# Cell sums and weight splits moved behind the block seams, a new order of matrix-block buffers, the last chunk's sums ahead of its value products, and kept blocks later in the sweeps

## The chip, the cores and the metric

The kernel runs on one core of one Trainium2 chip. Its engines are TensorE (PE in the rows; its weight loads are PEld), VectorE (DVE), ScalarE (ACT), GpSimd (POOL) and SyncE (SP). Each works through its own queue in order; SP issues nearly all DMA transfers here. The metric is the device time of one execution in microseconds (us), less is better. The kernel before takes 1789.12 us (median of 3 runs, 1788.32 to 1796.11). The profiled execution, from which all rows come, took 1783.08 us.

## What is computed

A sequence of 2048 rows of 640 numbers passes through four layers, each with a layer norm ahead and a residual sum behind: A, B, A, B.

```python
def _A_ref(x, wqkv, wo):          # H = 32 heads of 20, window W = 8, dilation 2
    qkv = (x @ wqkv)...           # q, k, v
    idx = pos[:, None] - off[None, :]      # off = 0, 2, ..., 14
    logits = einsum("bhsd,bhswd->bhsw", q, k[idx]) * scale
    logits = where(idx >= 0, logits, -1e9)
    o = einsum("bhsw,bhswd->bhsd", softmax(logits), v[idx])
    return o.reshape(B, S, D) @ wo
def _B_ref(x, Cr, Ci, Dr, Di):
    a, b = x @ Dr.T, x @ Di.T
    return Cr @ a - Ci @ b
x = x + _A_ref(layernorm(x), wqkv, wo)
x = x + _B_ref(layernorm(x), ...)
x = x + _A_ref(layernorm(x), wqkv, wo)
x = x + _B_ref(layernorm(x), ...)
```

## The kernel before

**Arithmetic.** Each operand of a product is split into a rounded upper half and the rest, and a product is three matmuls (`PASSES`: upper by upper and the two mixed ones). So each tile that PE multiplies costs a copy on ACT (the upper half) and a subtraction (the lower half) on DVE or POOL ("a split", L127 and L131 for weights).

**Layer A** (`layer_a`, the first at about 0 to 396 us, the second at about 860 to 1277) goes over 4 chunks `c` of 512 rows, each of 4 tiles `j`. Its order is written out by hand: `at(step, phase, fn)` puts a piece of work into one of 67 steps, and inside a step the phases run in the order of `PHASES`. All engines keep to that order. A query/key/value product (L363) is evacuated by ACT (L370, tile `stg`), stored to memory (L379, L380) and read back as windows `win` (L418) and queries `qs`; ACT copies the queries into a bank (`q_copy`, L405); DVE multiplies queries by keys (L432) and probabilities by values (L472); POOL sums the products (L435, and L491 to L493); DVE does the reductions and the softmax (L442 to L467); ACT the exponential (L450). Output tiles are transposed on PE (L328), split by ACT (L332), a subtraction on PE (`pc_sub`, L336) and ACT (L351), multiplied by the output weights (`wo_mm`, L516) and added to the residual by DVE (`wo_add`, L160), which also frees the product's bank.

**Layer B** multiplies by the sequence matrix first. Its first output tile of two (`z_mm`, L963, t = 0) is computed inside the tail of layer A: 16 blocks of the sequence matrix, of 15 matmuls each, in thirds of five that `ZTHIRDS` gives to steps. In the first layer B (`li` = 1) a block is loaded raw (`c_load`, L919), split by ACT (`c_hi`, L923) and by POOL or DVE (`c_lo`, L950); blocks that were split before are kept in memory (`c0b`) and read back (`c_get`, L941), which is what the second one does with all of them. A split block sits in one of three buffers `s0`, `s2`, `s3` in turn (`c_tag`, L912); a raw one in one of two buffers `stg`, which the evacuations of layer A use too. `run` then evacuates the first tile (`zt_put`, L1018 to L1023), loads the hidden weights (`load_w`, L127 to L131), computes the second tile block by block, and among that work forms sums of cells of the normalised input (`x_whole`, L1086, and `x_combine`, L1094 to L1097). The rest of the output is computed by three `pair`s with seven products in place of eight (L1130), each in three sweeps over `NP` = 8 blocks, whose raw blocks come from memory (L1113) and are split by L1123 and L1124. In the first layer B the last sweeps of the pairs also split and store ten blocks in all for the second one (`c_keep`, list `KEEP`).

**Between the layers.** The last pair of the first layer B runs inside the second layer A (`early`), with hooks at its last sweep that load, normalise, transpose (L226) and split (L233, L237) the first tiles and load the first weights.

**Who sets the order.** In layer A the plan does, for all engines. In `run`, `pair` and `early` only PE's order is by hand; for the other engines the framework chooses from its own forecast, and `tc.issue_after(x)` keeps what is under it behind instruction `x`.

## Time and profile before

| | |
|---|---|
| median of the runs | 1789.12 us (1788.32 to 1796.11) |
| profiled execution | 1783.08 us, span 1781.3 us, mean granted PE clock 0.995 |
| PE busy | 1740.1 us (98%), 8798 matmuls |
| DVE, ACT, POOL busy | 1386.1 (78%), 813.7 (46%), 622.1 us (35%) |
| DMA | 425.15 MB, 239 GB/s on the mean |

A row of the timeline gives start and length in us, engine, line, operation, output and input tiles, tile of the array, shape and count; in square brackets the idle time of the engine before it and the instruction or transfer that ended it. A row of a group gives, behind the count, the busy time in us and the mean in ns, then the idle time ahead of the group's instructions with what ended it. A row of stretches gives the window, its length, for each engine the busy time and the count, the granted clock of PE (1.00 is full speed), the mean busy share of the DMA engines and GB/s.

### The profile page before, as it was taken

Reading aid. Unit: us, or ns where it says so; the run is one execution under the profiler, and the core shown is the slowest. Engines: PE = TensorE matmul, PEld = TensorE weight load, DVE = VectorE, ACT = ScalarE, POOL = GpSimd, SP = SyncE. Lnnn points to the kernel's source line nnn. Section 1 sums busy time; section 2 is a strip of 40 time slices with the busy share of each in tenths; the row PEclk is TensorE's granted clock in tenths of the full one; section 3 lists DMA queues with packets and bytes.
Section 4 is the critical chain, followed back from the end, with each engine's and each line's share of the span. In section 5 each row is a group of like instructions: output and inputs, shape, how many; then the busy total and the mean of one; then the engine's idle time right before and its main releaser. Section 6 shows DMA issues by size and latency. Waiting matters only on the chain.

```text
span 1781.3 us, 26451 instructions
## 1 busy us (share of the span) xinstructions
PE 1740.1 (98%) x8798; PEld 1505.6 (85%) x8798; DVE 1386.1 (78%) x2133; ACT 813.7 (46%) x1690; POOL 622.1 (35%) x585
## 2 busy tenths in 40 slices
PE   9999998999999999999999999999899999999999
PEld 7889887778888888888888889987788888888888
DVE  6999999987867767767738999989777677677683
ACT  4664544454444445445624344444434443443441
POOL 4899999840000000000017999989200000000000
PEclk9999998999999999999999999999999999999999
DMA  7896678758777687778737866687688767767761
GB/s 248 286 313 206 212 209 281 251 180 293 265 255 256 238 271 252 244 265 257 228 117 223 273 207 224 214 299 267 212 287 277 252 219 238 258 224 231 254 207 52
DMA packets 271849, 425.15 MB, mean 239 GB/s; under 512 B 22592, under 2 KB 150592, under 8 KB 271456
## 3 DMA queue, kind: packets, MB, share of 16 engines
q1 hardware_dynamic: 268512, 421.49, 71.8%
q10 hardware_dynamic: 3200, 1.97, 0.4%
q8 instruction: 70, 1.15, 0.3%
q14 instruction: 67, 0.55, 0.1%
HBM read 338.23 MB, written 85.14 MB: 238 GB/s over the span
## 4 chain that ended last, share of the span: by engine, by line
PE 60%; DVE 18%; DMA 10%; POOL 5%; issue 4%; ACT 2%; SPq 1%; DVEq 0%; ACTq 0%; POOLq 0%
PE aux L1041 13%; PE m L363 11%; PE m L1130 10%; PE t L1130 10%; PE pq L1130 5%; PE xt L1130 5%; DVE pr L432 4%; PE aux L516 3%; DVE pr L472 3%; DMA xc<-stg 3%; DMA win<-cs_in 2%; DVE lg L442 2%; POOL pr L491 2%; POOL pr L435 1%; POOL pr L492 1%
## 5 line engine op out<-in xcount | busy, mean ns | idle before, releaser
L363 PE MATMUL m<-r,s 128*128 128x480 f32 x1920 | 436.4, 382 | 2.8 <-ACT s L233 2.3
L363 PEld LDWEIGHTS m<-r,s 128*128 128x128 f32 x1920 | 355.2, 188 | 56.6 <-ACT s L233 3.2
L1123 ACT CAST r<-win 128x512 fp32r<-128x512 f32 x248 | 151.2, 619 | 168.4 <-DVE win L1159 81.5
L1041 PE MATMUL aux<-r2a,zo 128*128 128x320 f32 x768 | 226.4, 310 | 0.0
L175 POOL TENSOR_TENSOR stats<-stats,mhalf 128x1 f32<-128x1 f32 (+1 forms) x40 | 29.2, 730 | 560.0 <-ACT stats L171 551.1
L491 POOL TENSOR_TENSOR pr<-pr 128x640 f32<-128x640 f32 x126 | 207.0, 1643 | 40.3 <-DVE pr L472 39.8
L1041 PE MATMUL aux<-pr,zo 128*128 128x320 f32 x704 | 208.2, 308 | 0.0
L1124 DVE TENSOR_TENSOR r<-win,r 128x512 fp32r<-128x512 f32 x248 | 167.5, 688 | 44.4 <-ACT r L1123 43.1
L432 DVE TENSOR_TENSOR pr<-pq,win 128x1280 f32<-128x1280 f32 x128 | 189.7, 1483 | 15.7 <-ACT pq L405 12.9
L472 DVE TENSOR_TENSOR pr<-pq,win 128x1280 f32<-128x1280 f32 x128 | 190.9, 1491 | 4.9
L435 POOL TENSOR_TENSOR pr<-pr 128x640 f32<-128x640 f32 x118 | 168.2, 1426 | 12.9 <-DVE pr L432 12.4
L1130 PE MATMUL m<-r,r 128*128 128x512 f32 x606 | 156.2, 392 | 0.7 <-DVE r L1124 0.7
L1041 PEld LDWEIGHTS aux<-r2a,zo 128*128 128x128 f32 x768 | 144.1, 188 | 2.0
L1130 PEld LDWEIGHTS m<-r,r 128*128 128x128 f32 x606 | 113.6, 188 | 26.3 <-DVE r L1124 1.0
L1041 PEld LDWEIGHTS aux<-pr,zo 128*128 128x128 f32 x704 | 132.2, 188 | 2.1
L1130 PE MATMUL t<-r,r 128*128 128x512 f32 x483 | 130.7, 393 | 2.0 <-issue 1.0
L963 PE MATMUL m<-s,r 128*128 128x512 f32 x384 | 119.3, 398 | 11.6 <-DMA s<-c0b 3.8
L963 PE MATMUL t<-s,r 128*128 128x512 f32 x384 | 118.4, 396 | 2.3 <-DVE ot L1023 1.5
L492 POOL TENSOR_TENSOR pr<-pr 128x320 f32<-128x320 f32 x126 | 112.3, 891 | 9.9
L442 DVE TENSOR_REDUCE lg<-pr 128x64 f32<-128x640 f32 (+1 forms) x128 | 110.5, 864 | 4.5 <-POOL pr L435 4.3
L1130 PEld LDWEIGHTS t<-r,r 128*128 128x128 f32 x483 | 90.5, 188 | 23.4 <-issue 1.5
L370 ACT COPY stg<-m 128x480 f32<-128x480 f32 x128 | 70.9, 554 | 81.4 <-PE m L363 61.3
(283 smaller groups left out, 3231.0 us busy)
## 6 DMA issues: line engine op xcount, KB each, us to landing
win<-cs_in SPq DMA_DIRECT2D x354, 256.0 KB, 4.2
r<-xc SPq DMA_DIRECT2D x240, 256.0 KB, 4.4
win<-kvb SPq DMA_DIRECT2D x96, 440.0 KB, 4.5
xa<-cs_in SPq DMA_DIRECT2D x122, 256.0 KB, 4.3
win<-kvb SPq DMA_DIRECT2D x64, 360.0 KB, 5.0
xc<-stg SPq DMA_DIRECT2D x40, 512.0 KB, 3.4
kvb<-stg SPq DMA_DIRECT2D x60, 320.0 KB, 4.5
xr<-xs SPq DMA_DIRECT2D x41, 320.0 KB, 3.2
```

Of the source, the lines that this page charges most:

```text
L363: nc.tensor.matmul(mt[g][:, : 3 * F], st[:, a, k], wq[q][:, b, k], start=n == 0, stop=n == 14)
L432: nc.vector.tensor_tensor(pr, q, wview(u, jp, 0, [[1, FE]]), op=ALU.mult)
L435: nc.gpsimd.tensor_tensor(pv[:, :, 0:10], pv[:, :, 0:10], pv[:, :, 10:20], op=ALU.add)
L442: nc.vector.tensor_reduce(lgs[u][:, 2 * jp : 2 * jp + 2].rearrange("p j w h -> p (j w h)"), prq.pop((u, jp)), axis=AX.X, op=ALU.add,)
L472: nc.vector.tensor_tensor(pr.rearrange("p j w (h d) -> p j w h d", d=DH), lgs[u][:, 2 * jp : 2 * jp + 2].unsqueeze(4).to_broadcast([P, 2, ...
L491: g.tensor_tensor(pr[:, :, 0:4], pr[:, :, 0:4], pr[:, :, 4:8], op=ALU.add)
L492: g.tensor_tensor(pr[:, :, 0:2], pr[:, :, 0:2], pr[:, :, 2:4], op=ALU.add)
L963: self.last = nc.tensor.matmul(self.z[t][k], self.xn[c][:, a, j, k * P : (k + 1) * P], self.ct[s][:, b], start=s == 0 and i == 0, stop=s = ...
L1041: self.last = nc.tensor.matmul(self.ym[e][:, :320], zt[(k, a, ri)][:, j2 * P : (j2 + 1) * P], w[:, e * 320 : (e + 1) * 320], start=(k, a, ...
L1123: nc.scalar.copy(hi, raw)
L1124: nc.vector.tensor_tensor(lo, raw, hi.bitcast(F32), op=ALU.subtract)
L1130: nc.tensor.matmul(bank, w(a, kb), hl[b], start=start and (a, b) == (0, 0), stop=stop and (a, b) == (1, 0),)
```

## The change

No operation is added or taken away but for six weight splits that go from DVE to POOL. What changes is the place of work in the queues:

- Layer A of the first pass, step 46: the two subtractions of `pc_sub` go to a new phase `peL2` behind the output products.
- `c_tag`: the buffers of the split blocks rotate as `s2`, `s3`, `s0` in both layers.
- Block 0 in the first layer is loaded and split one step earlier; the upper half of block 3 goes to a new phase `chi` behind the copies of the output tiles. `ZTHIRDS` of the first layer gives a third of block 2 to step 52, and thirds of step 52 run ahead of that step's output products (both layers).
- Last chunk (`c` = 3): the residual loads move to step 58, `wo_add` to phase `sA` (ahead of the softmax parts and the value products on DVE), and its statistics and norms one step earlier.
- `run`: `x_whole` and `x_combine` stand behind the last evacuation of the first tile.
- `pair`: the kept blocks (up to four in a pair) are split and stored at blocks 2 to 5 of the last sweep rather than at 0 to 3.
- `early`: the transposes use other banks and hooks, and loads and splits of the weights of query groups 1 to 3 move into the plan of the second layer A, steps -7 to 1; odd ones split on POOL (`wq_split`).

```diff
@@ -44,9 +44,10 @@
 
 
 LEAD2 = (-7, -6, -5, -4, -2, -1, 0, 0, 1, 1, 2, 3, 3, 4, 5, 5)
+WSTEP = (0, 0, 0, 1, 1, 2, 2, 3, 3, 4, 4, 5, 5, 6, 7)
 WHOLE = ((43, 45, 47, 49, 51, 55, 57, 59), (51, 57))
 ZTHIRDS = (
-    {49: 3, 50: 3, 51: 2, 53: 3, 54: 1, 56: 3, 57: 6, 58: 3, 59: 4, 60: 2, 61: 1, 62: 3, 63: 4, 64: 1, 55: 0, 52: 0},
+    {49: 3, 50: 3, 51: 2, 52: 1, 53: 2, 54: 1, 56: 3, 57: 6, 58: 3, 59: 4, 60: 2, 61: 1, 62: 3, 63: 4, 64: 1},
     {50: 3, 51: 5, 52: 1, 53: 1, 54: 1, 55: 1, 56: 5, 57: 4, 58: 3, 59: 3, 60: 1, 61: 1, 62: 4, 63: 2, 64: 4},
 )
 TA = 65
@@ -301,7 +302,7 @@
                 pieces[step] = []
                 at(step, "peT0", pc_pe, step)
                 at(step, "hi", pc_hi, step)
-                at(step, "peL", pc_sub, step)
+                at(step, "peL2" if first and step == 46 else "peL", pc_sub, step)
                 at(step, "actL", pc_lo, step)
             pieces[step].append((kind, c, j, k0, k1, bank, col, tag))
 
@@ -555,6 +556,11 @@
         def wq_split(q, k):
             split(wq[q][:, 0, k], wq[q][:, 1, k], wq[(q, k)], eng=nc.gpsimd if k % 2 else None)
 
+        def wq_late(q, k):
+            if k == 0:
+                wq_begin(q)
+            wq[(q, k)] = wq_load1(q, k)
+
         def wo_raw(i):
             if i == 0:
                 wo_s["w"] = T([P, 2, KD, D], "r2a", F32R)
@@ -586,8 +592,8 @@
                 with tc.issue_after(prev.dma.ins):
                     wq[0] = a_weights_q(0)
 
-            def xt(j, part):
-                xt_pe(0, j, part, "pq")
+            def xt(j, part, bank="pq"):
+                xt_pe(0, j, part, bank)
                 xt_hi(0, j, part)
                 xt_lo(0, j, part)
 
@@ -597,17 +603,19 @@
                 {
                     2: lambda: (x_get(0), x_get(1)),
                     4: lambda: xt(0, 0),
-                    5: lambda: (xt(0, 1), x_get(2)),
-                    6: lambda: xt(1, 0),
-                    7: lambda: (w0(), xt(1, 1), x_get(3)),
-                    ("y", 1): lambda: xt(2, 0),
-                    ("y", 2): lambda: xt(2, 1),
-                    ("y", 3): lambda: xt(3, 0),
-                    ("y", 4): lambda: xt(3, 1),
+                    5: lambda: x_get(2),
+                    6: lambda: xt(0, 1),
+                    7: lambda: (w0(), xt(1, 0), x_get(3)),
+                    ("y", 0): lambda: xt(1, 1),
+                    ("y", 1): lambda: (xt(2, 0, "xt"), xt(2, 1, "t0")),
+                    ("y", 2): lambda: xt(3, 0),
+                    ("y", 3): lambda: xt(3, 1, "xt"),
                 },
             )
-            for q in range(1, NQ):
-                wq[q] = a_weights_q(q)
+            for i, (q, k) in enumerate((q, k) for q in range(1, NQ) for k in range(KD)):
+                st = LEAD2[0] + WSTEP[i]
+                at(st, "dmaw", wq_late, q, k)
+                at(st + 1, "misc", wq_split, q, k)
 
         def zero_rows():
             zrow = wtile([4, (W - 1) * FE])
@@ -788,13 +796,14 @@
                     tp(60 if j < 2 else 67, "o", c, j, 3, 5, "aux0" if j < 2 else "pq", 256 * (j % 2))
                 if j < len(w):
                     if xtags:
-                        at(w[j], "dmar", r_load, c, j, xtags[j])
+                        at(58, "dmar", r_load, c, j, xtags[j])
                     at(w[j], "pe3w", wo_mm, c, j, ("aux1", "aux0") if c == 3 else ("aux0", "aux1"))
-                    at(w[j] + 1, "misc", wo_add, c, j)
-                    at(w[j] + 2, "actl", wo_stats, c, j)
-                    at(w[j] + 3, "fin", wo_fin, c, j, j + 1)
-                    at(w[j] + 3 + (c == 2), "actl", handoff.ln_hi_own, c, j, xr, nstats)
-                    at(w[j] + 4 + (c == 2), "misc", handoff.ln_lo, c, j)
+                    d = c == 2
+                    at(w[j] + 1, "misc" if d else "sA", wo_add, c, j)
+                    at(w[j] + 1 + d, "actl", wo_stats, c, j)
+                    at(w[j] + 2 + d, "fin", wo_fin, c, j, j + 1)
+                    at(w[j] + 2 + 2 * d, "actl", handoff.ln_hi_own, c, j, xr, nstats)
+                    at(w[j] + 3 + 2 * d, "misc", handoff.ln_lo, c, j)
         for ph in ("peT0", "hi", "peL", "actL"):
             plan.pop((67, ph))
         at(66, "pe3w", wo_mm, c, 2, ("aux0", "aux1"), 0, 2, 0, 3)
@@ -818,13 +827,14 @@
             if first and z in PRE:
                 at(max(thirds[3 * z - 7] + 1, t - 3), "dmac", handoff.c_get, z)
             elif first:
+                t -= z == 0
                 at(t - 2, "dmac", handoff.c_load, z)
-                at(t - 1, "hi", handoff.c_hi, z)
+                at(t - 1, "hi" if z != 3 else "chi", handoff.c_hi, z)
                 at(t - 1, "misc", handoff.c_lo, z, z < NJ or z in (11, 12))
             else:
                 at(min(t - 1, 48 + z) if z < 3 else t - 1, "dmac", handoff.c_get, z)
             for p in range(3):
-                at(thirds[3 * z + p], "pe3", handoff.z_mm, z, p)
+                at(thirds[3 * z + p], "pe2" if thirds[3 * z + p] == 52 else "pe3", handoff.z_mm, z, p)
         if first:
             at(62, "dmac", handoff.c_load, 13)
             at(63, "hi", handoff.c_hi, 13)
@@ -833,7 +843,7 @@
             at(63, "dmac", handoff.c_get, 13)
 
         PHASES = (
-            "peT0 dma evac hi pe peL pe2 fin red0 dma2 qk sA sB av0 sD red1 sE sC exp evacA actL evacO actl sF av1 qc actz"
+            "peT0 dma evac hi pe peL pe2 peL2 fin red0 dma2 qk sA sB av0 sD red1 sE sC exp evacA actL chi evacO actl sF av1 qc actz"
             " dmaw dmas misc dmac dmar pe3w pe3"
         ).split()
         with tc.manual_schedule(engines=ENGINES):
@@ -910,9 +920,8 @@
 
         def c_tag(self, s, t=0):
             if t:
-                return (("s3", "s0") if self.li == 1 else ("s0", "s3"))[s % 2]
-            tags = ("s3", "s0", "s2") if self.li == 1 else ("s2", "s0", "s3")
-            return tags[s % 3] if s < NST - 1 else "s1"
+                return ("s3", "s0")[s % 2]
+            return ("s2", "s3", "s0")[s % 3] if s < NST - 1 else "s1"
 
         def c_load(self, s, t=0):
             self.raw[s] = T([P, 512], "stg", bufs=2)
@@ -1017,10 +1026,14 @@
             for o, r in pieces[0]:
                 nc.scalar.copy(o, z[:, r])
             if len(pieces[0]) == len(pieces[1]) == 1:
-                nc.vector.tensor_tensor(pieces[1][0][0], z, pieces[0][0][0].bitcast(F32), op=ALU.subtract)
+                self.low = nc.vector.tensor_tensor(
+                    pieces[1][0][0], z, pieces[0][0][0].bitcast(F32), op=ALU.subtract
+                )
             else:
                 for r in range(2):
-                    nc.vector.tensor_tensor(zt[(k, 1, r)], z[:, r], zt[(k, 0, r)].bitcast(F32), op=ALU.subtract)
+                    self.low = nc.vector.tensor_tensor(
+                        zt[(k, 1, r)], z[:, r], zt[(k, 0, r)].bitcast(F32), op=ALU.subtract
+                    )
 
         def evac(self, t):
             self.zt_new(t)
@@ -1247,8 +1260,8 @@
                     self.product(f2, self.x_plain(*k1(i), 512), p12, False, i == NP - 1)
                     c6 = split(combine(b11, b11, b12, ALU.add))
                     self.product(m6, x6, c6, *ends)
-                    if self.li == 1 and i < len(KEEP[p]):
-                        self.c_keep(KEEP[p][i], views, tags)
+                    if self.li == 1 and 2 <= i < 2 + len(KEEP[p]):
+                        self.c_keep(KEEP[p][i - 2], views, tags)
                     if i > 2:
                         self.ymm(t1, 0, i - 3, i - 2)
                     hook(i)
@@ -1274,7 +1287,7 @@
         def run(self, nstats):
             self.evac(0)
             self.load_w()
-            todo = []
+            low, todo = self.low, []
             for i in range(0, NP, 2):
                 todo += [(self.x_whole, (side, i)) for side in (2, 0)]
                 todo += [(self.x_combine, (m, i)) for m in XC]
@@ -1287,8 +1300,9 @@
                     if s == 13:
                         self.ymm(0, 1, 0, 2)
                     if s > 1:
-                        for fn, args in todo[:3]:
-                            fn(*args)
+                        with tc.issue_after(low.ins):
+                            for fn, args in todo[:3]:
+                                fn(*args)
                         todo = todo[3:]
                 assert not todo
                 self.ymm(0, 1, 2, KD)
```

## The prediction

> **What bounds the kernel now.** I read the page's totals first, then PE's waits, then PE in order of time round each place that the diff touches, then the other engines at those places. All line numbers are those of the kernel before.
>
> ```profile
> span 1781.3 us, 26451 instructions
> PE 1740.1 (98%) x8798; PEld 1505.6 (85%) x8798; DVE 1386.1 (78%) x2133; ACT 813.7 (46%) x1690; POOL 622.1 (35%) x585
> ```
>
> TensorE is busy 1740.1 of 1781.3 us, and the change leaves every matmul in place. So all that it can win is idle PE time, 41.2 us, and matmuls that ran at a lower clock. The idle time lies in short gaps. These are the ones at the touched places (start, length, instruction, count, then the idle time before it and its releaser):
>
> ```profile
> 263.26 0.83 PE L336 MATMUL t<-s,nident 128*128 128x256 f32 x2 [1.79 <-ACT s L332]
> 280.92 1.42 PE L963 MATMUL m<-s,r 128*128 128x512 f32 x5 [1.71 <-POOL s L950]
> 298.10 2.24 PE L516 MATMUL aux<-r2a,ot 128*128 128x320 f32 x7 [2.05 <-ACT s L351]
> 354.07 6.21 PE L516 MATMUL aux<-r2a,s 128*128 128x320 f32 x30 [2.82 <-DVE xa L160]
> 374.34 2.91 PE L516 MATMUL aux<-r2a,zo 128*128 128x320 f32 x18 [0.18 <-ACT zo L351]
> 398.96 0.94 PE L963 MATMUL t<-s,r 128*128 128x512 f32 x3 [0.75 <-DVE ot L1023]
> 400.30 0.94 PE L963 MATMUL t<-s,r 128*128 128x512 f32 x3 [0.39 <-DVE ot L1020]
> 573.78 0.49 PE L1130 MATMUL xt<-r,r 128*128 128x512 f32 x1 [0.49 <-ACT r L1123]
> 575.12 0.73 PE L1130 MATMUL xt<-r,r 128*128 128x512 f32 x2 [0.85 <-DVE r L1124]
> 583.42 1.43 PE L1130 MATMUL m<-r,r 128*128 128x512 f32 x5 [0.72 <-DVE r L1124]
> 863.51 0.55 PE L226 MATMUL pq<-ident,xa 128*128 128x128 f32 x3 [0.94 <-DVE s L237]
> 890.21 2.46 PE L363 MATMUL m<-r,s 128*128 128x480 f32 x10 [0.67 <-ACT s L233]
> 897.74 2.44 PE L363 MATMUL m<-r,s 128*128 128x480 f32 x10 [1.66 <-ACT s L233]
> 1179.19 0.73 PE L963 MATMUL m<-s,r 128*128 128x512 f32 x2 [2.58 <-DMA s<-c0b]
> 1235.30 4.67 PE L516 MATMUL aux<-r2a,s 128*128 128x320 f32 x30 [0.41 <-DVE xa L160]
> 1246.88 0.73 PE L963 MATMUL m<-s,r 128*128 128x512 f32 x2 [1.23 <-DMA s<-c0b]
> 1280.22 0.93 PE L963 MATMUL m<-s,r 128*128 128x512 f32 x3 [2.25 <-DVE zo L1023]
> 1282.62 0.93 PE L963 MATMUL t<-s,r 128*128 128x512 f32 x3 [0.76 <-DVE ot L1023]
> 1283.95 0.93 PE L963 MATMUL t<-s,r 128*128 128x512 f32 x3 [0.40 <-DVE ot L1020]
> ```
>
> The 18 gaps other than the 0.18 sum to 22.5 us, 1.3% of the run. Between these places PE runs without a pause, so what is won at one is kept. Whether a gap can be won depends on what its releaser itself waited for.
>
> **The change, place by place.**
>
> **A, first layer, 264 to 303.** By stretch (us, then busy time and count of PE, PEld, DVE, ACT, POOL, the granted clock, DMA share, GB/s), then ACT and DVE in order of time, and the group of DMA issues (count, KB each, median us to landing):
>
> ```profile
> 264.00:303.00 39.00, 33.02 (x162) 28.21 (x161) 36.62 (x53) 19.66 (x48) 35.85 (x34) 0.87 0.89 290
> ```
> ```profile
> 290.00:294.00 4.00, 2.60 (x12) 2.33 (x13) 3.93 (x6) 1.74 (x7) 3.03 (x4) 0.84 0.96 328
> ...
> 298.00:302.00 4.00, 3.90 (x15) 3.90 (x15) 3.65 (x6) 3.84 (x8) 3.84 (x4) 0.50 0.96 334
> ...
> 354.00:358.00 4.00, 3.93 (x16) 3.93 (x17) 3.93 (x8) 0.35 (x2) 3.84 (x5) 0.57 0.68 220
> ...
> 1180.00:1184.00 4.00, 4.00 (x16) 3.26 (x14) 1.81 (x3) 0.16 (x1) 3.85 (x4) 0.57 1.04 388
> ```
> ```profile
> 270.64 0.42 ACT L405 COPY pq<-qs 128x320 f32<-128x320 f32 x1
> ...
> 274.10 0.62 ACT L923 CAST s<-stg 128x512 fp32r<-128x512 f32 x1 [0.35 <-DMA stg<-cs_in]
> ```
> ```profile
> 272.16 1.48 DVE L432 TENSOR_TENSOR pr<-pq,win 128x1280 f32<-128x1280 f32 x1
> ```
> ```profile
> stg<-cs_in SPq DMA_DIRECT2D x8, 256.0 KB, 4.8
> ```
>
> Here DVE is the bound (36.62 of 39 us) and PE is not (33.02). So moving the two L336 subtractions of step 46 behind 15 products removes PE's 1.79 but shortens nothing by itself: 0. Against it stands the earlier block 0. Its load now precedes two key/value loads on SP and its cast L923 precedes the query copy L405 on ACT. The load's buffer is a store's buffer, so it cannot start sooner; the cast still waits for the landing, at 274.10. L405 then runs at about 274.7 to 275.1 rather than 270.64, and DVE's L432 at 275.1 rather than 272.16: +2.9, less some 0.5 of slack that DVE has in the 2.4 us it idles here: +2.4. Behind it on ACT wait L370 and four L332 copies, so PE idles from about 272 to 276. On SP the two key/value loads wait some 6 us for that buffer and land about as DVE needs them: 0 to 0.3. The cast's lower half on POOL (L950) moves ahead of L435 on an engine that is 35.85 of 39 busy; it removes the 1.71 and delays the sums by its 1.3, both inside DVE's bound. A third of block 2, five matmuls, moves into the gap before 298.10: -1.2, since five take 1.42 in the row at 280.92 with their drain. At 298 the clock is 0.50: seven L516 took 2.24 (0.32 each) where 18 took 2.91 at full speed (0.16 each), which doubles some 2.4 us of products. With the gaps round 290 differently spread I take 2.2 of that as saved. Sum 2.4 - 1.2 - 2.2 = -1.0. Ends: all of the delay hidden, -3.4; the load landing in its group's 4.8 instead of the 2.6 it took here, and the clock still low, 2.4 + 2.2 - 1.2 = +3.4.
>
> [...]
>
> **B, first layer, last chunk.** The sums L160 that free the product banks move ahead of the value products:
>
> ```profile
> 353.53 0.48 DVE L160 SCALAR_TENSOR_TENSOR xa<-aux,xa 128x320 f32<-128x320 f32 x1
> ```
> ```profile
> 353.69 1.55 POOL L491 TENSOR_TENSOR pr<-pr 128x640 f32<-128x640 f32 x1 [1.84 <-DVE pr L472]
> ...
> 366.27 1.93 POOL L491 TENSOR_TENSOR pr<-pr 128x640 f32<-128x640 f32 x1 [0.62 <-DVE pr L472]
> ```
>
> PE's 2.82 ahead of 354.07 goes, and the 0.57 clock after it probably, worth half of 3.4 us, 1.7. But L472 then starts two L160 later (1.0), and POOL, which sums behind it without a pause from 353.69 to some 366, becomes what PE waits for. I take -1.5. Ends -4.5 (both kept) and +1.0 (only the delay of L472). The earlier residual load costs SP two issues, under 1 us, and no one waits for them.
>
> **C and H, the two block seams (398, 1280).** The changed order puts L1086 (1.22 us on DVE) behind the last evacuation:
>
> ```profile
> 1277.82 0.74 ACT L127 ACTIVATE r2a<-xa 128x640 fp32r<-128x640 f32 x1 [2.31 <-DMA xa<-wre_in]
> ...
> 1280.59 1.22 DVE L1086 TENSOR_TENSOR s<-r 128x1024 f32<-128x1024 f32 x1
> ```
>
> Gaps 0.75 + 0.39 and 0.76 + 0.40 go: -1.1 each (ends -1.3, 0). The 2.25 stays: there ACT waits for a weight load that the change leaves where it was. What slides later is feed for pairs that start some 75 us on.
>
> **D, kept blocks at blocks 2 to 5 of a pair's last sweep, not 0 to 3.** The gaps at 573 to 583 lie in the first blocks of such a sweep. By stretch, as above:
>
> ```profile
> 570.00:580.00 10.00, 8.66 (x40) 6.76 (x40) 5.20 (x9) 3.54 (x7) 0.32 (x1) 1.00 1.02 357
> 590.00:600.00 10.00, 10.00 (x54) 8.83 (x53) 4.26 (x8) 1.72 (x4) 0.00 (x0) 1.00 0.56 185
> ```
>
> Where the gaps are, DMA is full (1.02) and DVE is not; some blocks later it is at 0.56. Moving four loads and eight stores there frees the early blocks: 0.49 + 0.85 + 0.72 = 2.1 at most; the later pairs' share I do not count. I take -1.8. Ends -2.6, and +2.5 if gaps of 0.85 come up at three later blocks.
>
> **E, early, 860 to 900.** Transposes move to other banks and one step forward, and 15 weight splits leave this stretch for layer A's plan:
>
> ```profile
> L131 DVE TENSOR_TENSOR r<-win,r 128x480 fp32r<-128x480 f32 x20 | 12.9, 657 | 6.2 <-ACT r L127 6.0
> L127 ACT ACTIVATE r<-win 128x480 fp32r<-128x480 f32 x20 | 11.8, 603 | 4.7 <-DMA win<-wqkv_in 3.6 <-PE m L1130 0.8
> ```
>
> L233 and L237, for which PE waits, no longer stand behind ACT and DVE work that waits for weights: 0.94 + 0.67 + 1.66 = -3.3. In layer A the second query group's products start near 909, its last split would end near 893 and the fourth group's near 932 against a need at 944; six go to POOL, which is idle there until 924. Ends -3.3 and -1.0.
>
> **F, G, second layer A.** The load of block 1 takes a buffer that is free about 2 us sooner, so SP issues the rest sooner, block 2's included:
>
> ```profile
> s<-c0b SPq DMA_DIRECT2D x22, 512.0 KB, 5.5
> ```
>
> Block 2 took some 6.7 us from its issue at 1172.5. Of its 2.58 I take 1.4 (ends 0 and -4.2, with the 0.57 clock behind it). In the last chunk the 0.41 goes, the 1.23 hangs on a load that stands behind the same store as before: -0.4 (ends -1.6, +1.5).
>
> **Sum.** -1.0 - 1.5 - 1.1 - 1.8 - 3.3 - 1.4 - 0.4 - 1.1 = -11.6 us. It is made on the profiled execution's 1783.08 us (span 1781.3); the median of the runs is 1789.12, 6.0 above, and I carry the difference over: 1777.5. The ends added singly are -22.2 and +7.4; as they are independent, the likeliest case's own range is 1773 to 1783.
>
> **The rivals.**
> 1. Transfers set what I give to order. Blocks 0 and 2 and the kept blocks wait for landings either way, so A, D and F give nothing: -7.4, 1781.7. For it: 0.35 and 2.58 "<-DMA", DMA share 0.89 to 1.04. Against: 0.56 after 590.
> 2. The clock never falls. B and F keep the 1.7 each, A goes to -3.4: -17.4, 1771.7. For it: the low stretches follow the gaps that go. Against: A's new idle time.
> 3. A's new idle time, 272 to 276 on PE, lowers the clock for a stretch of 3.4 us, and the 298 one stays: A is +1.2 + 1.7 = +2.9, sum -7.7, 1781.4. [...]
> 4. DVE and POOL hold A and B, and D and F return as other gaps, so only C, E, H count: -5.5, with half of E lost to late weights -3.8: 1785.3. For it: DVE 3.93 of 4 at 354.
> 5. Slower: the block load holds ACT more than once. The two store buffers are shared, so each of blocks 0 to 3 has its cast in front of a query copy and stalls DVE by 2.9 + 2.2 = 5.1, with no slack left. Four times is +20.4, sum -10.6 + 20.4 = +9.8, 1798.9. It decides from the third stall on (10.6 / 5.1 = 2.1). For it: DVE is the bound there. Against: only block 0 moves.
>
> **How the numbers follow.** Chances: forecast 0.38, rivals 0.24, 0.12, 0.08, 0.11, 0.07. Half a per cent, about what a measurement of this kernel can tell from no change, is 8.9 us, so the limit is 1780.2. Faster: 0.7 of the forecast, all of rival 2, a quarter of rivals 1 and 3: 0.27 + 0.12 + 0.08 = 0.47. Slower: rival 5 and a little for the unforeseen, 0.08. Same: 0.45. The range 1771 to 1789 leaves out rival 5 and the far sides.
>
> **What would show it.** Right: no gap at 263, 863, 890, 897 and 399; no L1086 between evacuations; L405 ending near 275 right behind L923; L160 before L472 at the last chunk; POOL named as PE's releaser near 366; DMA share below 1 in 570 to 580. Wrong: PE idle at blocks 2 to 5 of the pairs' last sweeps, L363 waiting for L131 after 905, L405 late at blocks 1 to 3, or low-clock stretches in new places.

## The result, and the profile after

The changed kernel takes 1775.44 us (median of 6 runs, 1771.79 to 1777.14) against 1790.32 us (6 runs, 1785.77 to 1796.11) for the kernel before beside it: 0.991, with a 95% interval of 0.9888 to 0.9933. Run once more beside other kernels it took 1773.24 us, 0.9925 (0.9909 to 0.994). So it is faster, by about 0.8 to 0.9%.

The profiled execution of the changed kernel took 1775.34 us. From the page of the changed kernel, and from its list of what PE waited for (us in total, number of waits, the longest):

```profile
span 1773.2 us, 26454 instructions
PE 1735.7 (98%) x8798; PEld 1504.2 (85%) x8798; DVE 1388.1 (78%) x2127; ACT 812.5 (46%) x1690; POOL 628.8 (35%) x591
```
```profile
PE xt L337 <- ACT ot L333: 5.9, 1, 5.9
PE m L972 <- POOL s L959: 3.9, 3, 2.1
PE aux L329 <- POOL zo L494: 2.8, 1, 2.8
...
PE m L972 <- DMA s<-c0b: 2.1, 2, 1.4
```

The two waits at the head of the old list, for c0b (3.8) and for POOL's L950 (3.7), are now 2.1 and 3.9 (L959, by the new line numbers); the third, 3.2 for L160 (2.82 of it in one gap), is gone. Two new waits stand in the list: 5.9 us for a cast L333, and 2.8 us for POOL's L494. In order of time on PE in the changed kernel:

```profile
277.26 0.69 PE L337 MATMUL xt<-ot,nident 128*128 128x384 f32 x1 [5.92 <-ACT ot L333]
...
371.50 0.66 PE L329 MATMUL aux<-ident,zo 128*128 128x128 f32 x4 [2.81 <-POOL zo L494]
...
399.71 0.97 PE L972 MATMUL t<-s,r 128*128 128x512 f32 x3 [0.23 <-DVE ot L1029]
...
580.79 0.74 PE L1143 MATMUL xt<-s,r 128*128 128x512 f32 x2 [0.91 <-DVE s L1137]
...
1143.40 0.82 PE L337 MATMUL t<-s,nident 128*128 128x256 f32 x2 [1.27 <-ACT s L333]
...
1173.36 0.74 PE L972 MATMUL m<-s,r 128*128 128x512 f32 x2 [0.70 <-DMA s<-c0b]
...
1270.51 0.93 PE L972 MATMUL m<-s,r 128*128 128x512 f32 x3 [0.93 <-DVE zo L1034]
...
1347.26 0.92 PE L1143 MATMUL t<-r 128*128 128x512 f32 x3 [1.11 <-DVE ot L1034]
```

Between 850 and 910 the list shows no gap at all. Where the time went is read by matching the two traces matmul by matmul: the start of the same-numbered matmul in both, and how that difference changes over each stretch (times are those of the kernel before; minus is time won). The second column of traces is the changed kernel's second execution, against the same trace of before.

| stretch | forecast | first | second |
|---|---|---|---|
| before 255 | 0 | +0.4 | +0.6 |
| A, 255 to 344 | -1.0 | +0.7 | 0.0 |
| B, 344 to 395 | -1.5 | -0.4 | -0.3 |
| C, 395 to 440 | -1.1 | -1.6 | -1.3 |
| 440 to 560 | 0 | +2.4 | +0.4 |
| D, 560 to 856 | -1.8 | -3.2 | -2.5 |
| E, 856 to 910 | -3.3 | -3.9 | -3.4 |
| 910 to 1165 | 0 | +1.8 | +0.3 |
| F, 1165 to 1190 | -1.4 | -3.5 | -3.1 |
| G, 1190 to 1262 | -0.4 | -0.9 | -0.9 |
| H, 1262 to 1290 | -1.1 | -2.5 | -0.4 |
| 1290 to end | 0 | +2.8 | +0.6 |
| sum | -11.6 | -8.1 | -10.0 |

The traces give 8 to 10 us, the medians 13 to 15. Both traces of the kernel before (1783.08 and 1783.72 us) come from executions that are short for it: of the 45 runs of it that stood beside the runs here (1779.16 to 1796.11) only 10 were as short as the second or shorter. So the traces may show somewhat less than the medians do.

### The profile page after: what moved, and what is told of

It is laid out like the page before. It is cut to its first block, busy times and chain, and to the rows that moved or that the text cites. A ratio compares the mean times of both kernels' runs of the same rounds, so it can differ in the third digit from the quotient of the medians.

```text
span 1773.2 us, 26454 instructions
## 1 busy us (share of the span) xinstructions
PE 1735.7 (98%) x8798; PEld 1504.2 (85%) x8798; DVE 1388.1 (78%) x2127; ACT 812.5 (46%) x1690; POOL 628.8 (35%) x591
## 3 DMA queue, kind: packets, MB, share of 16 engines
q10 hardware_dynamic: 3200, 1.97, 0.4%
## 4 chain that ended last, share of the span: by engine, by line
PE 62%; DVE 15%; POOL 9%; DMA 8%; issue 3%; ACT 2%; SPq 0%; DVEq 0%; ACTq 0%; POOLq 0%
PE m L364 13%; PE aux L1054 13%; PE t L1143 10%; PE m L1143 10%; PE pq L1143 5%; PE xt L1143 5%; POOL pr L492 3%; DVE pr L433 3%; DMA xc<-stg 3%; DVE pr L473 3%; PE aux L517 2%; POOL pr L436 2%; POOL pr L493 2%; DVE lg L443 1%; DMA win<-cs_in 1%
## 5 line engine op out<-in xcount | busy, mean ns | idle before, releaser
L364 PE MATMUL m<-r,s 128*128 128x480 f32 x1920 | 436.3, 382 | 0.5 <-DVE r L644 0.2
L364 PEld LDWEIGHTS m<-r,s 128*128 128x128 f32 x1920 | 355.5, 188 | 54.1 <-DVE r L644 1.0
L433 DVE TENSOR_TENSOR pr<-pq,win 128x1280 f32<-128x1280 f32 x128 | 189.8, 1483 | 13.7 <-ACT pq L406 11.4
L473 DVE TENSOR_TENSOR pr<-pq,win 128x1280 f32<-128x1280 f32 x128 | 190.7, 1491 | 5.0
L972 PE MATMUL m<-s,r 128*128 128x512 f32 x384 | 118.8, 396 | 8.9 <-POOL s L959 3.9
L972 PE MATMUL t<-s,r 128*128 128x512 f32 x384 | 117.7, 394 | 0.4 <-DVE ot L1029 0.4
```

Of the source, the lines that this page charges most:

```text
L364: nc.tensor.matmul(mt[g][:, : 3 * F], st[:, a, k], wq[q][:, b, k], start=n == 0, stop=n == 14)
L433: nc.vector.tensor_tensor(pr, q, wview(u, jp, 0, [[1, FE]]), op=ALU.mult)
L473: nc.vector.tensor_tensor(pr.rearrange("p j w (h d) -> p j w h d", d=DH), lgs[u][:, 2 * jp : 2 * jp + 2].unsqueeze(4).to_broadcast([P, 2, ...
L972: self.last = nc.tensor.matmul(self.z[t][k], self.xn[c][:, a, j, k * P : (k + 1) * P], self.ct[s][:, b], start=s == 0 and i == 0, stop=s = ...
```

## The experiments

All edits are to the changed kernel, if nothing else is said, and lines are the changed kernel's (a line or two less where an edit shortens it). Medians are compared inside one group of runs, which shared a chip. In the first group the kernel before had 1783.98 us, in the second 1786.67, in the third 1785.76.

**1. The kernel before, a second trace.** No edit.

> The kernel before once more, for a second trace. Theory: one execution differs from another by where the low-clock stretches fall, because gaps of 2 to 3 us lie near what halves the clock; the gaps themselves come back within 0.3 us in the same places, and the low stretches (17 us in the first trace) differ by at least one of 3.4 us. Rival: the executions differ by the landing of transfers, so the gaps behind transfers (1179, 1246, 1280) change by a microsecond or more and the low stretches stay.

1783.72 us. PE's gaps stand in the same places but are not the same within 0.3 us: 1.78 before 263.32 (was 1.79), but 0.57 at block 0 (was 1.71), 1.77 before 861.92 (was 0.94), 3.22 before c0b at 1178.90 (was 2.58). PE's timeline and two stretches of this trace:

```profile
263.32 0.82 PE L336 MATMUL t<-s,nident 128*128 128x256 f32 x2 [1.78 <-ACT s L332]
...
1178.90 0.95 PE L963 MATMUL m<-s,r 128*128 128x512 f32 x2 [3.22 <-DMA s<-c0b]
```
```profile
264.00:268.00 4.00, 4.00 (x18) 3.96 (x17) 3.79 (x6) 1.41 (x4) 4.00 (x3) 0.57 0.93 256
...
299.00:302.00 3.00, 3.00 (x13) 3.00 (x13) 2.93 (x5) 2.94 (x4) 2.84 (x4) 0.50 0.96 351
```

The clock fell after the gap of 1.78 us here (0.57 over 264 to 268), and not after the one of 1.79 in the first trace (1.00 over the same 4 us). Both theories hold in part: the gap behind the transfer at 1179 moves by 0.64 us and others by up to 1.14, and the low stretches move. Their sum was 17 us both times. Matched like the table, the two traces of this one kernel differ by up to 1.9 us in a stretch. A difference of a microsecond or two at one place between two traces proves nothing by itself.

**The changed kernel, a second trace.** No edit.

> The changed kernel once more, beside the others of this call on the same chip. Theory: it stays 8 to 16 us below the kernel before, and the loss of 2.5 us at 1345 to 1400 (gaps of 1.1 and 0.8 us and 3.4 us of low clock), which the traces of two of its variants do not have, comes in some executions only. Rival: that loss belongs to the changed kernel and comes again.

1773.24 us (1770.14 to 1773.39), 0.9925 (0.9909 to 0.994). The two gaps near 1347 come again (0.58 and 0.83 us), the low clock behind them (0.66 over 1349 to 1354 in the first trace) does not; that stretch, 1345 to 1400, costs 0.7 us here and 2.8 in the first trace. So the gaps belong to the kernel and the larger part of the loss to the execution.

**2. Block 0 of the first layer, late again.**

```diff
             elif first:
-                t -= z == 0
                 at(t - 2, "dmac", handoff.c_load, z)
```

> The changed kernel with block 0 of the first layer loaded and split one step later, as before. Theory: the cast of block 0 on ACT, which waits for its transfer, holds the query copy, DVE's L433 idles 3.6 us, PE 5.9 us and the clock falls for 6.8 us; without it these go, the stretch 256 to 303 gets 2 to 3.5 us shorter than in the changed kernel, and the total is near 1772.5 us. Rival: DVE's and POOL's own work sets the end of this stretch, the old gaps (1.7 behind POOL at block 0) come back, and the total stays at 1775 within 1 us.

1769.54 us (1766.91 to 1773.22), 0.9919 (0.9904 to 0.9934). The trace is 3.1 us ahead of the kernel before at 303, where the changed kernel was 1.4 and 1.0 behind: 4.0 to 4.5 us for this one step there. ACT and DVE of the changed kernel, then ACT and PE of this one:

```profile
275.39 0.62 ACT L932 CAST s<-stg 128x512 fp32r<-128x512 f32 x1 [3.74 <-DMA stg<-cs_in]
275.91 0.42 ACT L406 COPY pq<-qs 128x320 f32<-128x320 f32 x1
```
```profile
276.37 1.49 DVE L433 TENSOR_TENSOR pr<-pq,win 128x1280 f32<-128x1280 f32 x1 [3.64 <-ACT pq L406]
```
```profile
270.70 0.42 ACT L406 COPY pq<-qs 128x320 f32<-128x320 f32 x1
...
274.32 0.62 ACT L931 CAST s<-stg 128x512 fp32r<-128x512 f32 x1 [1.19 <-DMA stg<-cs_in]
```
```profile
272.05 0.44 PE L337 MATMUL xt<-ot,nident 128*128 128x384 f32 x1 [1.12 <-ACT ot L333]
```

In the changed kernel ACT waits 3.74 us for the block, the query copy follows it at once, DVE waits 3.64 us for the copy and PE 5.92 for the casts behind it. With the block late the copy runs at 270.70, PE waits 1.12, and the clock is 1.00 from 262 to 300 (0.92 from 262 to 305 in the changed kernel). The gap of 1.67 behind POOL's L958 at block 0 does come back, as the rival said, but does not set the end. Over 255 to 344 the two traces with the block late (this one and run 11's) win 3.5 and 3.6 us on the kernel before; the ten other traces of the changed kernel and its variants lie between 1.3 won and 0.8 lost, so the step is worth 2.2 to 4.4 us at its place. The medians do not show it: 0.9919 lies between the changed kernel's 0.991 and 0.9925.

**3. Block 0's cast in another phase.** The load stays early.

```diff
-                at(t - 1, "hi" if z != 3 else "chi", handoff.c_hi, z)
+                at(t - 1, "hi" if z not in (0, 3) else "chi", handoff.c_hi, z)
```

> The changed kernel, block 0 loaded early as it is there, but its cast on ACT in the phase behind the copies of the output tiles instead of ahead of the query copy. Theory: it is the cast's place on ACT, not the early load on SP, that stalls DVE; with the load early and the cast late, DVE's wait of 3.6 us at its L433 and PE's 5 to 6 us at 271 go, and 256 to 303 is as short as with the load late (3.4 us below the kernel before at 303). Rival: the load on SP, which holds two key/value loads behind it for 6 us, is the cause; then DVE waits for a window instead of the queries and the stretch stays 0.5 to 1.5 us longer than before.

1773.28 us, 0.993 (0.9916 to 0.9943), not to be told from the changed kernel. ACT and DVE of this kernel:

```profile
274.55 0.62 ACT L932 CAST s<-stg 128x512 fp32r<-128x512 f32 x1 [3.46 <-DMA stg<-cs_in]
275.07 0.42 ACT L406 COPY pq<-qs 128x320 f32<-128x320 f32 x1
```
```profile
275.53 1.49 DVE L433 TENSOR_TENSOR pr<-pq,win 128x1280 f32<-128x1280 f32 x1 [2.88 <-ACT pq L406]
```

The edit misses its aim: in `PHASES` the query copy's phase `qc` comes after `chi`, so the cast still stood ahead of it. The run repeats the changed kernel's mechanism (cast waits 3.46, DVE waits 2.88 for the copy) and tells the two causes apart only in this: DVE is released by the copy, not by a window, in all these traces. The load itself hardly moves on SP (issued at 271.53 in the kernel before, 272.45 in the changed one, 271.60 in run 2), but in the changed kernel two loads of windows go out behind it, at 272.88 rather than 265.50. What that costs by itself stays open: a kernel with the load early and the cast behind the copy was not run.

**4. The cell sums free again.**

```diff
-                        with tc.issue_after(low.ins):
-                            for fn, args in todo[:3]:
-                                fn(*args)
+                        for fn, args in todo[:3]:
+                            fn(*args)
```

> The changed kernel without the order of the cell sums behind the last evacuation in run. Theory: only the two seams pay, 1.2 us near 398 and 2.5 us near 1275, so the total is 3.7 us longer, near 1779 us. Rival: the sums that slid later cost the changed kernel 1.9 us at 440 to 480 and 2.6 us at 1345 to 1360 (DVE behind PE); undone, these come back as a gain and the total stays at 1775 within 1 us.

1781.23 us, 0.9984 (0.9973 to 0.9995). Undone, this one step takes nearly the whole gain; the trace ends 10.0 us behind the changed kernel's. DVE of this kernel in both layers' last chunks, then PE there:

```profile
369.65 1.80 DVE L1099 TENSOR_TENSOR s<-r 128x1024 f32<-128x1024 f32 x1
...
371.78 1.49 DVE L473 TENSOR_TENSOR pr<-pq,win 128x1280 f32<-128x1280 f32 x1
...
1249.86 1.77 DVE L1099 TENSOR_TENSOR s<-r 128x1024 f32<-128x1024 f32 x1 [1.37 <-PE t L972]
...
1252.17 2.89 DVE L473 TENSOR_TENSOR pr<-pq,win 128x1280 f32<-128x1280 f32 x2
```
```profile
372.83 0.66 PE L329 MATMUL aux<-ident,zo 128*128 128x128 f32 x4 [3.69 <-POOL zo L494]
...
1256.90 0.33 PE L329 MATMUL pq<-ident,zo 128*128 128x128 f32 x1 [2.27 <-POOL zo L494]
```

Left free, the sum L1099 is put into the last chunk of both layers, ahead of value products L473; in the second layer it waits there 1.37 us for a product (L972, which reads `s`). The output tiles come later (3.69 us of idle time before 372.83 against 2.81 in the changed kernel, 2.27 before 1256.90, where the changed kernel has no such gap), and the clock fell behind that: 10.2 us of low clock between 373 and 387, where the changed kernel has 3.4 (0.66 over 373 to 378), and 6.8 us from 1257.41 (0.68 over 1256 to 1260, then 0.50 to 1264); over the whole run the mean granted clock is 0.992 against the changed kernel's 0.996. From 366 to 402 this kernel loses 5.0 to 5.4 us more than the two traces of the changed one, from 1250 to 1290 4.5 to 6.6. Both expectations fall: the step is worth some 10 us, not 3.7, and not 0.

The kernel before has one such sum inside the last chunk of the second layer too. DVE there:

```profile
1255.36 1.65 DVE L1086 TENSOR_TENSOR s<-r 128x1024 f32<-128x1024 f32 x1
1256.93 2.37 DVE L488 TENSOR_REDUCE zo<-pr 128x160 f32<-128x1280 f32 x1
```

So where the free sums go is not fixed: it changed when the work round them did.

**5. Step 46 behind the products in both layers.**

```diff
-                at(step, "peL2" if first and step == 46 else "peL", pc_sub, step)
+                at(step, "peL2" if step == 46 else "peL", pc_sub, step)
```

> The changed kernel with the subtractions of step 46 behind the output products in the second layer A too. Theory: PE, some 5.6 us ahead of DVE there since 860 to 900, meets DVE's pace at 1142 and loses 1.27 us waiting for the casts; with the products first that gap goes and the total is 1.3 us shorter, near 1774. Rival: DVE binds from there on, the gap only moves behind the products, and the total stays within 0.3 us.

1771.65 us, 0.9933 (0.9914 to 0.9952), not to be told from the changed kernel's 0.991 and 0.9925. Its trace has no gap at the place of the 1.27; but the changed kernel's second trace has none there either. Inconclusive.

**6. The last chunk's sums as before.**

```diff
-                        at(58, "dmar", r_load, c, j, xtags[j])
+                        at(w[j], "dmar", r_load, c, j, xtags[j])
...
-                    at(w[j] + 1, "misc" if d else "sA", wo_add, c, j)
+                    at(w[j] + 1, "misc", wo_add, c, j)
...
```

Statistics and norms behind it go back too.

> The changed kernel with the last chunk's sums, norms and residual loads in their old places. Theory: the sums ahead of the value products won 3.0 us of idle time and a low clock of 3.4 us at 351, and POOL's chain gave most of it back (2.8 us idle at 368 and 3.4 us of low clock behind it), so undoing them moves the total by less than 1 us. Rival: the early sums are worth what the first gaps say, and undoing them costs 3 to 4.5 us.

1773.77 us, 0.9933 (0.9913 to 0.9953), against the changed kernel's 1773.24 in the same group. PE of this kernel, and a stretch behind the gap:

```profile
354.30 6.20 PE L517 MATMUL aux<-r2a,s 128*128 128x320 f32 x30 [2.43 <-DVE xa L161]
```
```profile
355.00:358.00 3.00, 3.00 (x13) 3.00 (x12) 2.93 (x4) 0.17 (x1) 2.84 (x4) 0.50 0.84 259
```

The old gap comes back with its low clock (0.50), and the new one behind POOL's L494 (2.81) with its own (0.66 over 373 to 378 in the changed kernel) is gone: over 344 to 395 the two kernels differ by 0.4 us. The early sums moved the wait from DVE to POOL.

**7. The kept blocks at blocks 0 to 3.**

```diff
-                    if self.li == 1 and 2 <= i < 2 + len(KEEP[p]):
-                        self.c_keep(KEEP[p][i - 2], views, tags)
+                    if self.li == 1 and i < len(KEEP[p]):
+                        self.c_keep(KEEP[p][i], views, tags)
```

> The changed kernel with the kept blocks at blocks 0 to 3 of the last sweeps again. Theory: their loads and stores fill the DMA engines where the sweep starts; the gaps near 570 to 583 (2.1 us) and 711 (0.6 to 0.9 us) come back and the total is 2.5 us longer than the changed kernel's. Rival: the transfers of the sweep itself set these gaps, and the total stays within 0.5 us.

1774.34 us, 0.9936 (0.9921 to 0.9952): 1.1 us above the changed kernel's median in the same group, inside what the runs can tell. PE of this kernel:

```profile
574.02 0.73 PE L1143 MATMUL xt<-r,r 128*128 128x512 f32 x2 [0.75 <-DVE r L1137]
...
711.37 0.73 PE L1143 MATMUL xt<-r,r 128*128 128x512 f32 x2 [0.86 <-DVE r L1137]
```

The gaps come back (1.3 us near 573 and 582, 1.4 near 711), and over 480 to 720 its trace loses 2.5 us more than the changed kernel's second one and 3.1 more than the first. That is what the theory says for the place, but two other traces speak against a firm size: the kernels of runs 3 and 10 keep the blocks late, and yet have gaps near 717 (run 3, on PE; 1.36 and 0.92 in run 10):

```profile
716.22 0.49 PE L1143 MATMUL xt<-s,r 128*128 128x512 f32 x1 [1.56 <-ACT s L1136]
717.63 0.73 PE L1143 MATMUL xt<-s,r 128*128 128x512 f32 x2 [0.92 <-DVE s L1137]
```

Over 560 to 856 they lose 0.4 and 1.6 us against the kernel before, as this run loses 0.4, while the nine other traces with the blocks late win 2.2 to 4.0. So the step gains in most executions and not in all. What it does not do is empty the DMA engines. The changed kernel at the first of these places:

```profile
572.00:582.00 10.00, 9.09 (x44) 7.49 (x43) 5.23 (x9) 4.05 (x7) 0.00 (x0) 1.00 1.01 349
```

They are as full as before (1.01, was 1.02), and one gap of 0.91 is left at 580.79.

**8 and 9. The two halves of the early stretch.** Weights back ahead of the plan (`wq_early`), or transposes in their old places (`xt_old`):

```diff
-            for i, (q, k) in enumerate((q, k) for q in range(1, NQ) for k in range(KD)):
-                st = LEAD2[0] + WSTEP[i]
-                at(st, "dmaw", wq_late, q, k)
-                at(st + 1, "misc", wq_split, q, k)
+            for q in range(1, NQ):
+                wq[q] = a_weights_q(q)
```
```diff
-                    5: lambda: x_get(2),
-                    6: lambda: xt(0, 1),
...
+                    5: lambda: (xt(0, 1), x_get(2)),
+                    6: lambda: xt(1, 0),
...
```

> The changed kernel with the weight splits of query groups 1 to 3 back ahead of the plan, the transposes in their new places. Theory: ACT and DVE work that waits for weights stands before the splits of the transposed tiles again, so the gaps of 0.67 and 1.66 us near 890 and 897 come back: 2.3 us longer than the changed kernel. Rival: the new banks and places of the transposes alone had removed them: within 0.5 us.

> The changed kernel with the transposes of the early stretch in their old banks and places, the weight splits in the plan. Theory, after the run that put the weights back and lost nothing: the places and banks of the transposes alone removed the gaps of 0.94, 0.67 and 1.66 us; with the old ones 1.5 to 3.3 us of them come back at 860 to 900, weights or no weights. Rival: either part alone is enough, so this kernel shows no gap over 0.7 us there either.

With the weights back: 1769.95 us (1769.16 to 1771.49), 0.9911 (0.9894 to 0.9927), and no gap between 855 and 905. With the old transposes: 1775.01 us, 0.9942 (0.9926 to 0.9959), and on PE

```profile
891.17 4.65 PE L364 MATMUL m<-r,s 128*128 128x480 f32 x13 [2.14 <-ACT s L234]
```

with a low clock of 3.4 us behind it (13 of these L364 took 4.65 us, where 10 took 2.36 at 883.27); over 856 to 910 it loses 0.4 us where the changed kernel wins 3.4 to 3.9. So the gain of this stretch is that of the transposes' banks and places (the two were not tried apart). Moving the weights gave nothing that shows; the median without it is even 3.3 us lower, though the intervals overlap.

**10. The old buffer order in the second layer.**

```diff
-            return ("s2", "s3", "s0")[s % 3] if s < NST - 1 else "s1"
+            tags = ("s2", "s3", "s0") if self.li == 1 else ("s2", "s0", "s3")
+            return tags[s % 3] if s < NST - 1 else "s1"
```

> The changed kernel with the old order of buffers in the second layer (s2, s0, s3). Theory: block 1 waits for s0 until 1168 on SP, the loads behind it go out later, and the gap behind block 2's transfer grows from 0.7 or 1.1 us to 2 to 2.6 us, with a low clock of 3.4 us behind it in some executions: 1.3 to 3.2 us longer at 1172 to 1190. Rival: that gap follows the load on the DMA engines whatever the buffers, and stays at about 1 us.

1775.24 us (1771.19 to 1780.28), 0.9932 (0.9918 to 0.9945). PE, and a stretch behind it:

```profile
1179.44 1.09 PE L973 MATMUL m<-s,r 128*128 128x512 f32 x2 [3.02 <-DMA s<-c0b]
```
```profile
1179.00:1183.00 4.00, 3.56 (x9) 2.80 (x10) 1.42 (x2) 0.00 (x0) 3.84 (x5) 0.58 1.05 391
```

The gap is 3.02 again (0.70 in the changed kernel) and the clock fell behind it, to 0.58 over these 4 us; over 1172 to 1190 it loses 0.3 us where the changed kernel wins 3.1 to 3.5. The three traces with the old order (two of the kernel before, this one) have 2.58, 3.22 and 3.02 us here; of the eleven with the new order ten have at most 1.11, and run 4's has 1.61. The order of buffers is the cause, as thought, though the times of whole runs do not resolve it.

**11. A version from the findings.** Block 0 late, step 46 behind in both layers, weights ahead of the plan: the edits of 2, 5 and 8 together.

> Three steps in one: block 0 late as before, the subtractions of step 46 behind the products in both layers, the weight splits ahead of the plan as before; all else as changed. Theory: the first is worth 3 to 4 us, the others 0 to 1 each, total near 1768 us, 0.988 to 0.990 of the kernel before. Rival: once PE is 12 us ahead, DVE's pace in the second layer A takes the rest back at 1140 to 1165, and the total is that of the changed kernel, 0.991 to 0.9925.

1768.58 us (1766.82 to 1771.59), 0.9903 (0.9891 to 0.9916). Beside it in the same group ran the kernel of run 3, which stalls as the changed kernel does, with 1773.28; the intervals just touch. Against the changed kernel's own runs (0.991 and 0.9925) the gain is not resolved. The trace ends 16.3 us ahead of the kernel before, where the changed kernel's end 8.1 and 10.0 ahead; but the traces of runs 2 and 5, each with one of the three edits, end 16.5 ahead, so that the three add up is not shown. All three traces are of the shortest execution of their kernel. The rival has its part too. PE of this kernel:

```profile
1158.77 0.44 PE L337 MATMUL t<-r,nident 128*128 128x384 f32 x1 [1.89 <-ACT r L333]
```

where the changed kernel waits 0.57: PE, further ahead, meets the pace of the attention there.

Not undone by themselves were step 46, the thirds of block 2 and the buffer order in the first layer.

## Why the prediction was right

The forecast was 1777.5 us, the time is 1775.44: the change is faster, by the mechanism of the forecast, gaps of PE closed one by one. That the total came so close is in part luck. The traces won 8.1 and 10.0 us of the 11.6, the medians 13 to 15, and the terms erred in both directions: A and B came out 2.8 and 2.2 us worse than forecast, D, E and F 4.1 and 2.5 us better, and the stretches taken as 0 cost 7.4 and 1.9 us.

- **A, the wrong sign.** The mechanism was read rightly: L406 ended near 276 right behind the cast, DVE stalled (3.64 us, the forecast had 2.9 less 0.5), PE idled. What failed is the step "I take 2.2 of that as saved": the clock did stay up at 298 (1.00 over 290 to 300), but fell instead at 274.6 for 6.8 us (0.50 over 275 to 280; 3.4 us in the second trace, 0.69 over the same 5 us), inside the new idle time of 5.92 us before 277.26. That is rival 3's first half, and the sign of being wrong that the forecast named as low-clock stretches in new places. A came to +0.7 and 0.0 instead of -1.0; with block 0 late it is -3.5 (run 2), so by the traces the early cast costs some 2 to 4 us.
- **B, mis-sized.** Taken as -1.5, measured -0.4 and -0.3. POOL became what PE waits for (2.81 us before 371.50; the forecast said near 366), and took back all but that; undoing the whole part changes nothing that the runs resolve (run 6).
- **C near its size (-1.6 and -1.3), H not (-2.5 and -0.4), against -1.1 each; and both wrong in what the step is worth.** In H the forecast let the 2.25 us behind L1023 stay; it was 0.93 in the first trace, and 1.97 with a low clock of 3.4 us behind it in the second (0.57 over 1270 to 1274). Undone, the step costs some 10 us, because the sums then go into the last chunk, which the forecast did not cost. And "what slides later is feed for pairs that start some 75 us on" was too easy. The slid sums now stand between the evacuations of the second tile, DVE of the changed kernel:

```profile
1344.96 0.69 DVE L1107 TENSOR_TENSOR stg<-s 128x512 f32<-128x512 f32 x1
...
1346.70 0.41 DVE L1034 TENSOR_TENSOR ot<-t,zo 128x256 fp32r<-128x256 f32 x1
```

  and PE waits 1.11 us for that L1034. At 440 to 560 and from 1290 on the change loses 2.4 and 2.8 us (0.4 and 0.6 in the second trace). Run 4, with the sums free, bears on this. At 440 to 560 its trace wins 1.2 us, where the eleven with the order lose 0.4 to 2.1 or, in one, 2.4; but the second trace of the kernel before is 1.3 us ahead there too. From 1290 on it loses 2.3, while ten of the eleven lie within 0.7 of the kernel before: that loss does not follow the sums, and 3.4 us of low clock stand behind it both in run 4 and in the changed kernel's first trace.
- **D, right for the changed kernel's traces:** -1.8 was taken, -3.2 and -2.5 came, run 7 gives 2.5 to 3.1 back; two variants with the same step win nothing there (run 7). The mark "DMA share below 1" was wrong: it is 1.01. So the gaps were not set by a full queue alone; which transfers set them was not looked at.
- **E, right in size** (-3.3; -3.9 and -3.4) **and wrong in cause.** I gave it to both halves, above all to the weights that no longer stand ahead of L233 and L237. Runs 8 and 9 give it to the transposes.
- **F, mis-sized.** 1.4 was taken, 3.5 and 3.1 came: with the gap at 0.70 or 1.11 the clock did not fall (1.00 over 1172 to 1190 in the first trace), and that was the other half, which I had kept for the far end. The way was as stated: SP issued block 1's load at 1162.16 instead of 1168.31, some 2.3 us more than PE's own lead of 3.8 there.
- **Between the places** the forecast held that PE runs without a pause and keeps what it wins. The first half was misread: the trace it rests on has gaps that its list leaves out, of 1.05 us before 475.74, 0.87 before 367.98, and the largest inside A:

```profile
291.40 0.73 PE L963 MATMUL m<-s,r 128*128 128x512 f32 x2 [2.03 <-POOL s L950]
```

  It stays in the changed kernel (2.13 before 295.76). The second half did not hold either: after 910 the changed kernel lost 1.8 us (0.3 the second time), mostly at 1143.40, where PE arrived ahead of the attention. A lead of some 6 us met the pace of the attention there in one trace and not in the other; one of 12 us (run 11) waits 1.89 at 1158.77.

On the clock the forecast took the low stretches to follow gaps such as the 2.82 us before 354.07, with 0.57 over 354 to 358 behind it. The runs bear that out in part: the clock fell behind single gaps of 1.78 (run 1), 2.14 (run 9) and 2.43 us (run 6, 0.50 over 355 to 358), but not behind the 2.25 before 1280.22 in the kernel before (1.00 over 1276 to 1292).

## What to carry to other kernels

On a kernel like this, whose bound engine is 98% busy, the gain lies in gaps of one or two microseconds, and each is priced by what its releaser was queued behind. A part of a change should be undone alone: here one part cost 2 to 4 us by the traces, two gave nothing that shows, and one carried most of the gain. A cast that waits for a transfer, put ahead of a copy that another engine waits for, stalled both engines here until the transfer landed (3.74 us on ACT and 3.64 on DVE). Where a scheduler places work freely, a constraint that keeps it behind a seam is worth what the work would do at the place where the scheduler puts it next, not only at the place where it stands now.

## What the runs showed of the hardware

In the trace of the kernel before, the granted clock of TensorE was at 0.50 for 10.2 us from 292.9, for 3.4 us from 354.3 and for 3.4 us from 1180.3; in the first trace of the changed kernel for 6.8 us from 274.6, for 3.4 us from 373.6 and for 3.4 us from 1349.8. Between these stretches both traces have 1.00. At 0.50 seven L516 took 2.24 us (0.32 each), at full speed 18 took 2.91 (0.16 each); by these two times 3.4 us of low clock cost at most 1.7 us, an estimate.

The length of a single gap does not tell by itself whether the clock fell behind it: it fell behind one of 1.78 us (run 1, 0.57 over 264 to 268), and not behind 1.79 (the kernel before, 1.00 over the same 4 us), 2.13 (the changed kernel before 295.76, 1.00 over 290 to 300) and 2.25 (the kernel before, before 1280.22). What decides was not shown. The sum of low clock is one way in which executions of one kernel can differ: the changed kernel's two traces have 13.7 and 10.2 us of it before their end, at a mean granted clock of 0.996 and 0.997.
